# Moving a cast, a set of transposes and three output steps in a hand-ordered attention and MLP kernel

## The chip, the cores and the metric

The kernel runs on one core of a Trainium2 chip. The metric is the device time of one execution in microseconds (us). The engines are TensorE (PE in the profile, its weight loads PEld), VectorE (DVE), ScalarE (ACT), GpSimd (POOL) and SyncE (SP). They run side by side and wait for each other by semaphores; each executes its own instructions in the order in which the program gives them.

## The reference

Eight batches of eight heads, 576 positions, head size 64. Heads 0 to 3 see the last 32 positions, heads 4 to 7 the positions with the same remainder modulo 32. The attention's output, 4608 rows of 512, goes through an MLP with a squared ReLU.

```python
scores = scale * np.matmul(q, k.transpose(0, 1, 3, 2))
mask_local = (rel >= 0) & (rel < stride)
mask_strided = (rel >= 0) & (pos[None, :] % stride == pos[:, None] % stride)
attn = softmax(np.where(masks, scores, -1e9))
x = np.matmul(attn, v).transpose(0, 2, 1, 3).reshape(4608, 512)
out = np.maximum(x @ w_in, 0.0) ** 2 @ w_out
```

## The kernel before

The attention works on units: a unit is a pair of heads of one batch, numbered 4 * batch + pair; pairs 0 and 1 are local, 2 and 3 strided. Its output is written, transposed, into four tiles `xt`, which are the moving operand of the MLP.

The MLP runs in nine chunks of 512 rows. A chunk is 16 groups `mm1` (four 128x512 products into one PSUM bank, L734; the relu `r` on ScalarE, L740; its square `g_sb` on VectorE, L741) and then 16 groups `mm2` (four products, L756; each fourth group ends an output tile `y`, evicted by ScalarE, L760, and stored from SP's queue, L764). Groups are numbered on: chunk 0's mm1 is 0 to 15 (0 to 4 are done earlier), its mm2 16 to 31, chunk 1's mm1 32 to 47, and so on; chunk 3 is 96 to 127. So a group's number says what it is.

The order of the work is written out by hand in the string `PLAN`. A line `n: words` says which attention steps are issued ahead of group n, in the order of the words; then the group is issued, and then what earlier steps put off with `later` (masks, squares). There is no planner: the place of a word sets the order on every engine and on every queue that the step uses. The words that matter here:

- `c9ka`, `c9kv`: cast of unit 9's k (a reordering copy from the loaded tile to `k_l`, L303), on ScalarE (a) or VectorE (v). Batch 2's local units are 8 and 9, batch 3's 12 and 13.
- `T9kv`: six transposes of it on TensorE into a bank (L480), copied by VectorE to `kTl` (L487).
- `S8!`: scores of a local unit, 12 small products into four banks (L532), four exponentials on ScalarE (L548), two masks put off on VectorE (L554).
- `D8.0`, `D8.1`: the two halves of the product with V (L694), a reciprocal and a product on VectorE (L699, L700). `E17` transposes such an output by a DMA from SP's queue (L709).
- `A12k`: transposing DMA of the cast k from SP's queue (L391).
- `U5`: loads of the strided heads' v into `v_st` (one buffer) from POOL's queue (L417, L420). `B40v`, `B41v`: spread of batch 4's v over `vb`, even and odd columns, on VectorE (L424).
- `C5k`, `X5k`: load of the strided k from POOL's queue (L355) and its transposing DMA from SP's (L360) into `kT_s`. `k50v`, `k51v`: copies of it to `kb` on VectorE (L371, L374).
- `s4.0` to `s4.2`: scores of batch 4's strided heads in three parts (L601), exponential (L602), mask (L604). `x4.0` to `x4.2`: the sums and the products with V (L612, L615) into two banks, Ln and Exp on ScalarE (L617, L618), and then six, six and four products on VectorE that copy the scaled output into `xt` (L625, L631).
- `G4`, `G5`: the scores of both local units of a batch at once, 24 products into six banks (L577), six exponentials (L588), masks (L584). `H4v` shifts part of v (L437).

Banks: `mm1` and `mm2` take turns on two banks; the attention steps take the oldest of a ring of six. A step waits until the step that had its bank six places earlier has been read. G takes all six.

Of the kernel before, what the change touches and what calls it, by code (L numbers as in the profile page):

```python
# [45 lines left out]
28: V3 E5a x1.2  # L46
29: c8kv
30: c8qv
31: c9ka c9qv
33: T8kv  # L50
34: C3q T8qv
35: T9qa
36: T9kv
38: C3k S8!
39: c12kv A12k
40: c13kv A13k
41: D8.0
42: D8.1 S9!
44: k20v E8 c12qv A12q
45: k21v D9.0 c13qv A13q  # L60
46: B20v D9.1
# [25 lines left out]
81: x3.0  # L87
83: x3.1
85: x3.2
93: H4v  # L90
94: G4
95: k40v
96: k41v B40v
97: Y20 Y21 B41v
98: U5
99: X5k D16.0 D16.1
100: C6k
# [6 lines left out]
107: D17.0  # L104
109: Q24k Q24q D17.1 s4.2
110: B50v
111: x4.0 B51v
112: E17
113: k50v
114: k51v x4.1  # L110
117: x4.2
121: G5
124: V6
127: H5v
128: U6
# [897 lines left out]
```

## Time and profile before

| what | us |
|---|---|
| three runs | 299.83, 300.20, 300.69; median 300.20 |
| the profiled execution | 300.21, its span 298.3 |
| TensorE busy | 289.8 (97%) |
| VectorE busy | 179.5 (60%) |
| ScalarE busy | 171.3 (57%) |
| GpSimd busy | 72.7 (24%) |
| share of TensorE in the chain that ended last | 83% |
| share of VectorE, DMA, ScalarE in it | 7%, 4%, 3% |

A timeline row has the start in us, the time in us, the engine, the line, the operation, output and input tiles, the shapes and how many instructions were merged; in brackets stand the engine's idle time before it and what ended that. `psb` is PSUM. A row of PEld is a weight load; the loads of a group are 0.216 us apart when nothing stands between. A row of SPq or a POOL row with DMA is the issue of a transfer, not the transfer. The list of DMA issues gives the time from issue to landing.

### The profile page before, as it was taken

What the parts mean: (1) busy time and instruction counts of PE and PEld (TensorE: products, weight loads), DVE (VectorE), ACT (ScalarE), POOL (GpSimd) and SP (SyncE); (2) the same over time, 40 slices, a digit from 0 to 9 for tenths busy, and PEclk for the clock granted to TensorE, in tenths of its full rate; (3) what the DMA queues carried; (4) which work ended last, traced back from release to release, by engine and by line L of the source; (5) the groups of instructions that cost most, each with busy time, mean ns of one, the idle gap of its engine ahead of it and who ended that gap; (6) DMA issues with size and microseconds to landing.
All of it is one profiled execution on the core that took longest, in us unless ns stands there. A gap on an engine that the chain in (4) does not pass through costs nothing.

```text
span 298.3 us, 5623 instructions
## 1 busy us (share of the span) xinstructions
PE 289.8 (97%) x2112; PEld 145.3 (49%) x2148; DVE 179.5 (60%) x465; ACT 171.3 (57%) x321; POOL 72.7 (24%) x107
## 2 busy tenths in 40 slices
PE   7989999999999999999999999999999999999995
PEld 3644555544544444454455445544454444444444
DVE  5657679686788585689367945786475534004400
ACT  3758846775677636764477447645665256217511
POOL 8874742005503007136304800000000000000000
PEclk9999999999999999999999999999999999999999
DMA  8999999999999999999998999411011100011012
GB/s 159 179 210 202 193 198 185 154 185 211 157 167 183 132 154 191 147 155 185 195 139 120 175 174 144 81 55 73 35 23 55 70 37 0 35 70 38 0 70 70
DMA packets 91722, 37.36 MB, mean 125 GB/s; under 512 B 77548, under 2 KB 85830, under 8 KB 91696
## 3 DMA queue, kind: packets, MB, share of 16 engines
q0 software_dynamic: 50608, 18.33, 58.1%
q1 hardware_dynamic: 40944, 18.62, 32.4%
q8 instruction: 16, 0.26, 0.4%
q10 hardware_dynamic: 144, 0.07, 0.1%
q14 instruction: 10, 0.08, 0.1%
HBM read 37.22 MB, written 9.44 MB: 156 GB/s over the span
## 4 chain that ended last, share of the span: by engine, by line
PE 83%; DVE 7%; DMA 4%; ACT 3%; issue 2%; POOL 0%; DVEq 0%; POOLq 0%; ACTq 0%
PE psb L734 38%; PE psb L756 32%; DVE xt L625 2%; DMA kT_s<-k_t 2%; DMA k_l<-in_k_dram 2%; PE psb L694 2%; PE psb L791 1%; PE psb L480 1%; PE psb L532 1%; PE psb L781 1%; PE psb L601 1%; ACT r L740 1%; DVE g_sb L741 1%; PE psb L615 1%; PE psb L612 1%
## 5 line engine op out<-in xcount | busy, mean ns | idle before, releaser
L734 PE MATMUL psb<-xt,w_in_b 128*128 128x512 bf16 x557 | 132.8, 379 | 1.4 <-ACT r L740 0.2
L756 PE MATMUL psb<-w_out_b,g_sb 128*128 128x512 bf16 x543 | 125.7, 379 | 1.2 <-DVE g_sb L741 0.4
L740 ACT ACTIVATE r<-psb 128x512 bf16<-128x512 f32 x144 | 85.3, 599 | 38.8 <-PE psb L734 33.1
L741 DVE TENSOR_TENSOR g_sb<-r 128x512 bf16<-128x512 bf16 x144 | 60.6, 423 | 69.9 <-ACT r L740 68.9
L734 PEld LDWEIGHTS <-w_in_b 128*128 128x128 bf16 x576 | 53.1, 98 | 58.9 <-issue 1.9
L756 PEld LDWEIGHTS <-g_sb 128*128 128x128 bf16 x560 | 52.1, 98 | 59.1 <-DVE g_sb L741 1.1
L760 ACT COPY y<-psb 128x512 f32<-128x512 f32 x35 | 20.6, 590 | 52.1 <-PE psb L756 47.3
L625 DVE TENSOR_TENSOR xt<-psb,rv 64x144 bf16<-64x144 f32 x84 | 34.0, 405 | 10.5 <-ACT rv L618 9.4
L617 ACT ACTIVATE rv<-psb 128x432 f32<-128x432 f32 (+1 forms) x21 | 10.5, 501 | 12.8 <-PE psb L612 12.8
L700 DVE TENSOR_TENSOR x_l<-psb,rinv 96x384 bf16<-96x384 f32 x28 | 15.5, 553 | 1.0
L355 POOL DMA_DIRECT2D q_t<-in_q_dram x6 | 3.2, 538 | 47.4 <-DMA qT_s<-q_t 46.3
L602 ACT ACTIVATE e<-psb 128x432 bf16<-128x432 f32 (+1 forms) x21 | 10.4, 496 | 4.1 <-PE psb L601 4.1
L284 POOL DMA_DIRECT2D k_l<-in_k_dram x16 | 11.9, 748 | 2.8 <-ACT rv L618 2.0
L631 DVE TENSOR_TENSOR xt<-psb,rv 64x270 bf16<-64x270 f32 (+1 forms) x28 | 10.9, 431 | 2.5 <-ACT rv L618 2.2
L588 ACT ACTIVATE e<-psb 128x384 bf16<-128x384 f32 x24 | 9.6, 509 | 3.4 <-PE psb L577 3.4
L618 ACT ACTIVATE rv<-rv 128x432 f32<-128x432 f32 (+1 forms) x21 | 11.2, 533 | 0.7
L284 POOL DMA_DIRECT2D q_l<-in_q_dram x16 | 11.6, 728 | 0.0
L584 DVE TENSOR_TENSOR e<-e,mask_all 128x576 bf16<-128x576 bf16 x16 | 6.7, 456 | 8.0 <-ACT e L588 8.0
L694 PEld LDWEIGHTS <-e 128*128 128x128 bf16 x168 | 8.7, 101 | 5.0
L694 PE MATMUL psb<-vl,e 128*128 128x65 bf16 x168 | 9.5, 195 | 0.0
L355 POOL DMA_DIRECT2D k_t<-in_k_dram x6 | 3.2, 536 | 25.1 <-DMA kT_s<-k_t 23.1
L615 PEld LDWEIGHTS <-vb 128*128 128x128 bf16 x154 | 7.1, 97 | 3.8
(120 smaller groups left out, 218.6 us busy)
## 6 DMA issues: line engine op xcount, KB each, us to landing
out_dram<-y SPq DMA_DIRECT2D x35, 256.0 KB, 2.8
w_out_b<-in_moe_w_out_dram POOLq DMA_DIRECT2D x4, 512.0 KB, 15.4
q_t<-in_q_dram POOLq DMA_DIRECT2D x7, 288.0 KB, 7.4
k_t<-in_k_dram POOLq DMA_DIRECT2D x7, 288.0 KB, 7.1
vl<-in_v_dram POOLq DMA_DIRECT2D x6, 288.0 KB, 7.2
v_st<-in_v_dram POOLq DMA_DIRECT2D x7, 216.0 KB, 7.1
w_in_b<-in_moe_w_in_dram POOLq DMA_DIRECT2D x2, 704.0 KB, 14.3
k_l<-in_k_dram POOLq DMA_DIRECT2D x16, 72.0 KB, 7.0
```

Of the source, the lines that this page charges most:

```text
L284: nc.gpsimd.dma_start(out=t[:, :, hh, :], in_=src[b, 2 * p + hh].rearrange("(t p) d -> p t d", p=QL))
L617: nc.scalar.activation(rv, pn, AF.Ln)
L618: nc.scalar.activation(rv, rv, AF.Exp, scale=-1.0)
L625: nc.vector.tensor_tensor(to[:, :, NJ * part:NJ * (part + 1), par], of, by, op=ALU.mult)
L631: nc.vector.tensor_tensor(t, of[:, g:, :, lo:lo + k], by[:, g:, :, lo:lo + k], op=ALU.mult)
L694: nc.tensor.matmul(po[0:m, n, :], e[:, c:c + m], rhs[:, NL * part + n, 0:D + 1], start=True, stop=True)
L700: nc.vector.tensor_tensor(x, po[0:QL, :, 0:D], rinv[0:QL].to_broadcast([QL, NL, D]), op=ALU.mult)
L734: nc.tensor.matmul(ph, w_in_b[:, kk, 128 * ff:128 * (ff + 1)], xt[kk][:, 512 * c:512 * (c + 1)], start=(kk == order[0]), stop=(kk == order ...
L740: nc.scalar.activation(r, ph, AF.Relu)
L741: later(1, lambda: nc.vector.tensor_tensor(g[:, ff, :], r, r, op=ALU.mult))
L756: nc.tensor.matmul(py, g[:, ff, 128 * j:128 * (j + 1)], w_out_b[:, ff, :], start=(ff == 0), stop=(ff == 15))
L760: nc.scalar.copy(y, py)
```

## The change

Only the plan's text is changed. Line 31 has the cast of unit 9's k on VectorE. Its transposes go from ahead of group 36 to ahead of group 39, behind the cast of 12's k and its transposing DMA, and so behind the scores of unit 8. At group 42 the scores of unit 9 go ahead of the second half of unit 8's product with V. The spread of batch 4's v goes from 96 and 97 to 88 and 89. The three parts of batch 4's strided output go from 111, 114, 117 to 113, 115, 118; the second spread of batch 5's v goes from 111 to 114, the scores of batch 5's local units from 121 to 122. E17 goes from 112 to 111.

```diff
-31: c9ka c9qv
+31: c9kv c9qv
 33: T8kv
 34: C3q T8qv
 35: T9qa
-36: T9kv
 38: C3k S8!
-39: c12kv A12k
+39: c12kv A12k T9kv
 40: c13kv A13k
 41: D8.0
-42: D8.1 S9!
+42: S9! D8.1
...
+88: B40v
+89: B41v
 93: H4v
 94: G4
 95: k40v
-96: k41v B40v
-97: Y20 Y21 B41v
+96: k41v
+97: Y20 Y21
 98: U5
...
 109: Q24k Q24q D17.1 s4.2
 110: B50v
-111: x4.0 B51v
-112: E17
-113: k50v
-114: k51v x4.1
-117: x4.2
-121: G5
+111: E17
+113: k50v x4.0
+114: k51v B51v
+115: x4.1
+118: x4.2
+122: G5
```

## The prediction

> **What bounds the kernel now.** I read the busy line and the clock row first, then the chain of waits, then the timeline of each place that the change touches, one engine at a time.
>
> ```profile
> PE 289.8 (97%) x2112; PEld 145.3 (49%) x2148; DVE 179.5 (60%) x465; ACT 171.3 (57%) x321; POOL 72.7 (24%) x107
> ...
> PEclk9999999999999999999999999999999999999999
> ```
>
> TensorE is busy 97% of 298.3 us at the full granted clock, so nothing but its own waits can be gained or lost. The profiled execution took 300.21 us (span plus 1.91 outside it); the median of the three runs is 300.20, so a sum made on one holds for the other. I call 0.3%, 0.9 us, what a measurement can tell from no change.
>
> A group is four 128x512 products; its first weight loads, without other work between, are 0.863 us apart. Where a plan word stands between, the surplus is its price; a larger surplus is a wait. Four waits lie near the edited words. Around groups 31 to 33:
>
> ```profile
> 50.77 0.59 ACT L760 COPY y<-psb 128x512 f32<-128x512 f32 x1 [0.28 <-PE psb L756]
> 51.26 0.83 ACT L303 COPY k_l<-xt 96x768 bf16<-96x768 bf16 x1
> 51.38 0.36 DVE L303 COPY k_l<-xt 96x768 bf16<-96x768 bf16 x1
> 51.99 0.58 ACT L760 COPY y<-psb 128x512 f32<-128x512 f32 x1
> ...
> 52.09 0.10 PEld L480 LDWEIGHTS <-k_l 96*128 96x128 bf16 x1
> ...
> 52.62 0.41 PE L480 MATMUL psb<-ident,k_l 96*128 96x96 bf16 x6 [0.16 <-ACT y L760]
> ```
>
> The cast of 9's k sits on ScalarE between two evictions; the second ends at 52.57, and the transposes of 8's k, which take its bank, start only then. Around groups 38 to 44:
>
> ```profile
> 58.66 1.31 ACT L548 ACTIVATE e<-psb 128x288 bf16<-128x288 f32 x4
> 59.83 1.13 ACT L740 ACTIVATE r<-psb 128x512 bf16<-128x512 f32 x2
> ...
> 60.52 0.53 PEld L734 LDWEIGHTS <-w_in_b 128*128 128x128 bf16 x3 [0.47 <-issue]
> ...
> 64.99 0.53 PEld L734 LDWEIGHTS <-w_in_b 128*128 128x128 bf16 x3 [0.29 <-issue]
> ```
>
> S8's four exponentials hold up the relu of group 38; its bank is wanted by group 40, which stands until 60.5. Group 44 does the same behind S9. Around groups 110 to 122:
>
> ```profile
> 132.46 2.50 DVE L625 TENSOR_TENSOR xt<-psb,rv 64x144 bf16<-64x144 f32 x6 [0.59 <-ACT rv L618]
> 134.99 0.52 DVE L424 COPY vb<-v_st 54x1408 bf16<-54x1408 bf16 x1
> 135.54 0.42 DVE L741 TENSOR_TENSOR g_sb<-r 128x512 bf16<-128x512 bf16 x1
> ...
> 140.03 1.57 DVE L631 TENSOR_TENSOR xt<-psb,rv 64x270 bf16<-64x270 f32 x4
> ...
> 136.02 0.76 PEld L756 LDWEIGHTS <-g_sb 128*128 128x128 bf16 x5 [0.84 <-DVE g_sb L741]
> ...
> 140.96 0.41 PEld L577 LDWEIGHTS <-kTl 64*128 64x128 bf16 x18 [0.42 <-issue]
> 141.66 0.18 PEld L577 LDWEIGHTS <-kTl 64*128 64x128 bf16 x6 [0.29 <-issue]
> ```
>
> The square of group 111 (135.54) is queued on VectorE behind the six products of x4.0 and a spread, and group 115 waits for it. Then G5's last third waits until the products of x4.2 end at 141.60.
>
> **The change, part by part.** All starts are of first weight loads, in the clock of the trace before.
>
> *c9k from ScalarE to VectorE.* It takes 0.83 us from ScalarE and gives VectorE 0.35 (51.65 to 52.00 for the same shape). The last eviction can then start when its product is done: earlier ones start 0.41 to 0.42 after the next group's first load (49.49 to 49.91, 50.36 to 50.77), so 51.22 gives 51.64, and its end 52.22. The transposes load at 52.09, and a transpose follows its load by 0.22 (53.52 to 53.74): 52.31 in place of 52.62, a gain of 0.31. Bounds: 0 (were the eviction not early) and 0.32, the whole surplus. On VectorE the cast goes ahead of 9's q, which is read at 54.4, and falls into an idle stretch of 0.86 before 53.13; without that cover it would delay the square of group 32 by 0.35, which is first read at group 48.
>
> *T9k behind S8.* A set of transposes costs TensorE 0.26: groups with one between start 1.12 apart (53.95, 55.08), 0.86 without. Ahead of S8 it is paid in full. After group 38 it lies in front of group 40's wait, which is 0.355 (60.52, where 59.95 + 0.216 was due) and ends with the relu of 38; that follows S8, so it moves by 0.31 + 0.26, and the wait shrinks to 0.10. Gain 0.26; bounds 0 and 0.26. Its 0.75 us copy on VectorE is now queued behind the square of 38 and the cast of 12's k (whose load lands at 58.08, needed at 60.3) and ends at 61.3 (square at 60.50 - 0.57, then steps of 0.34, 0.27 and 0.75). S9's loads come 1.00 after group 41's (86.71 to 87.71 at group 66), 61.53 - 0.57 + 1.00 = 61.96, so 0.6 to spare. Behind the copy wait a mask, three squares, 13's cast and the outputs of D8.0 and D8.1; with the steps of the trace (0.37, 0.34 each, 0.27, 0.70 each) S9's first mask ends at 64.8, against 65.07 (65.64 - 0.57) when D9.0 loads it: the next to be late. The transposes take the bank of 8's q, S8 one bank earlier in the ring; all were emptied before.
>
> *S9 before D8.1.* S9's exponentials cannot start before the relu of group 41 leaves ScalarE (62.64 to 63.24, they start at 63.13), so group 44's wait of 0.17 stays: 0, between 0.17 gained and 0.17 lost, since D8.1 then follows with its masks long ready.
>
> *V's spread of batch 4 to 88 and 89.* Two copies of 0.52 on VectorE leave 116.7 and 118.4 and go behind x3.2's products and ahead of the shift at 109.64. VectorE then idles 0.74 for the k of batch 4 (110.87) and 3.76 before 115.15; the k goes 0.3 later and is read after 123. No TensorE wait ends on the copies: 0; were the cover gone, 1.04 us on G4's masks, first read after 118.6. They also free v_st: the two loads of batch 5's v on POOL's queue, at 119.26 after a wait of 1.18 for the second copy, can go at 118.1. No DMA issue changes its place in either queue.
>
> *x4 and G5.* With x4.0 out of the way before group 111, group 112 starts at 131.27 (130.40 + 0.863). Its square is ready at 132.7 and is read at 135.3: the first wait, 0.53 (134.65 to 136.03 is 1.39 for 0.86), goes. VectorE then runs k50v at 132.75 to 133.5; x4.0 stands after group 112, its Ln starts 1.46 after that group's first load (132.52 to 133.98), 132.73, and its products 1.15 after that (131.31 to 132.46), 133.88. Then six products 2.50, k51v 0.80, the spread 0.55, six 2.50, four 1.57: the end is 141.8, against 141.60 before. G5, one group later, would reach its last third at 141.67 (131.27; nine groups 7.77; x4's parts 0.40, 0.40 and 0.30, the surplus of groups 110-111, 113-114 and 116-117; the group with G5 1.79, as G4's; less 0.25 from the last third to the next group) and waits until 141.9: 0.22 of wait, where the second wait had been 0.34. Gain 0.53 + 0.34 - 0.22 = 0.65; bounds 0.86, with no wait left, and 0.3, if VectorE is 0.35 slower. E17's DMA, moved from 112 to 111, keeps its place in SP's queue: it is issued at 132.47, when E16's, at 130.48, lets it.
>
> Sum: 0.31 + 0.26 + 0 + 0 + 0.65 = 1.22 us. After group 123 I find no wait of TensorE in the trace of before that could take it back; DMAs land early (batch 4's k at 110.84 for use after 123, qT of batch 5 at 134.07 for use at 154). 300.2 - 1.2 = 299.0.
>
> **The rivals.**
>
> *One half only.* If the head start of 0.57 is lost again before group 64, since VectorE is nearly without gaps from 65 to 72 (the chain runs along it there) and the copy of T9k now sits just ahead, the time is 300.2 - 0.65 = 299.55. Against it: the last square is ready at 71.57 and its weight load is at 72.60. If instead the x4 stretch stays bound by VectorE, 300.2 - 0.57 = 299.6; for it: VectorE is busy 14.45 of 17 us there.
>
> *Nothing moves.* TensorE meets the next late releaser in both places: 300.2. For it, only that each wait removed here had another engine close behind; the margins above (0.6, 0.3, 1.0 us) speak against it.
>
> *Slower: k50v in front of x4.0.* It now heads the queue that G5 waits for, and reads a DMA transpose issued at 126.79.
>
> ```profile
> 119.26 0.54 POOL L417 DMA_DIRECT2D v_st<-in_v_dram  x1 [1.18 <-DVE vb L424]
> ...
> kT_s<-k_t SPq DMA_TRANSPOSE x1, 4.0
> ...
> 131.33 0.53 POOL L355 DMA_DIRECT2D k_t<-in_k_dram  x1 [10.89 <-DMA kT_s<-k_t]
> ```
>
> It landed after 4.0 us, at 130.78, and k50v would start at 132.75, or 132.2 with the head start; another 0.35 is spare before x4.0's products. Other transposes of this tile took up to 11.2. At 11.2 it would land at 138.0, x4.0 would start at 138.8, 4.9 later, and the whole time would be 300.2 - 1.2 + 4.9 = 303.9. It costs something from a landing 1.75 us late, and decides the sign from 2.9 us late. For it: the v loads, 1.2 us earlier, share the DMA engines with the five transposes issued one after another from 121.50 on. Against it: those loads end at 126.27 even now, before this transpose is issued, and the next load is issued only after it has landed. The Trainium skill, page "DMA: Bandwidth & Descriptors", section "Issuing engines are not separate DMA queues", says that DMAs of all issuing engines run on the same 16 DMA engines and interleave. By that rule an earlier load slows the transposes ahead of this one; the trace agrees that company costs, with 10.2 us for the same transpose at 53.06 among loads and 4.0 alone.
>
> **How the numbers follow.** Both gains hold: 0.64, 299.0, own range 298.6 (no wait left, and 0.17 at group 44) to 299.4. One half only: 0.16, 299.6. Nothing: 0.06, 300.2. Slower: 0.14, up to 303.9; for such a shuffle many small releasers can come late, so I give it more than the margins alone would. The range 298.6 to 300.2 leaves out the slower case and a little below. Faster by over 0.3% (below 299.3): 0.64 and 0.02 of the halves, 0.66; within: 0.14 + 0.06, 0.20; slower: 0.14.
>
> **What would show it.** The transposes after group 32 start at their load plus 0.22 with no wait on the eviction; group 40's wait is near 0.1; group 115 has none; the products of x4.0 start 1.4 later against group 110 and G5's last third waits 0.2 for x4.2. Wrong would be: VectorE idle before k50v, S9 waiting for kTl, D9.0 waiting for its mask, or G5 standing longer than before.

## The result and the profile after

| | before | changed |
|---|---|---|
| median of six runs, us | 300.27 | 299.09 |
| lowest and highest | 299.83, 300.69 | 298.81, 299.58 |
| span of the profiled execution | 298.3 | 297.7 |
| its own time | 300.21 | 299.36 |

The ratio is 0.9962, with a 95% interval of 0.9949 to 0.9975: 1.1 us less, between 0.75 and 1.5. The forecast was 299.0. In later runs some executions, of the kernel before as of the others, had a lower granted clock and took about 2% longer; the ratios and medians leave them out.

The two spans differ by 0.6 only, and the starts of the groups tell why. I read the first weight load of each group in both traces (first loads, as in the prediction) and take the difference. Group 20, which no edit touches, starts 0.87 later in this profiled execution: its chain of waits begins with a load of v that the other's does not have.

```profile
5.53 8.30 DMA vl<-in_v_dram
13.83 0.02 issue
13.85 0.49 DVE vl L438
```

That is not the change: over the fourteen traces of this study, whose programs do not differ up to group 30, group 32 starts between 0.04 earlier and 0.77 later than in the first trace. So starts are compared from group 32 on, set to zero there. The changed kernel then stands like this against the one before:

| group | 33 | 39 | 41 | 45 | 110 | 123 | 283 |
|---|---|---|---|---|---|---|---|
| us | -0.32 | -0.14 | -0.58 | -0.58 | -0.58 | -1.38 | -1.38 |

Three steps, 0.32, 0.26 and 0.80, each at a place that the prediction named, and nothing is given back after. (At 39 the moved transposes have just been issued, and the wait that they shorten comes in group 40. Line numbers of the changed kernel are one higher; those of the other kernels shift with the number of lines in their plans.) First, the timeline of the changed kernel around group 32:

```profile
51.55 0.59 ACT L761 COPY y<-psb 128x512 f32<-128x512 f32 x1 [0.28 <-PE psb L757]
...
52.41 0.59 ACT L761 COPY y<-psb 128x512 f32<-128x512 f32 x1 [0.28 <-PE psb L757]
...
52.71 0.35 DVE L304 COPY k_l<-xt 96x768 bf16<-96x768 bf16 x1
52.86 0.49 PEld L481 LDWEIGHTS <-k_l 96*128 96x128 bf16 x6
...
53.08 0.42 PE L481 MATMUL psb<-ident,k_l 96*128 96x96 bf16 x6
```

The last eviction waits for its product now (0.28 of idle, PE), not for the cast; the transposes follow their load by 0.22 without a wait. Then the weight loads of groups 38 to 44:

```profile
58.62 0.55 PEld L735 LDWEIGHTS <-w_in_b 128*128 128x128 bf16 x4
59.28 0.48 PEld L481 LDWEIGHTS <-k_l 96*128 96x128 bf16 x6
...
60.72 0.53 PEld L735 LDWEIGHTS <-w_in_b 128*128 128x128 bf16 x3 [0.21 <-issue]
...
62.73 0.28 PEld L533 LDWEIGHTS <-kTl 64*128 64x128 bf16 x12 [0.42 <-DVE e L555]
...
65.19 0.53 PEld L735 LDWEIGHTS <-w_in_b 128*128 128x128 bf16 x3 [0.29 <-issue]
```

9's transposes lie after group 38, and the idle time in group 40 is 0.21 where it was 0.47; that of group 44 is 0.29 as before. Last, VectorE and the weight loads from group 111 to 122:

```profile
132.51 0.43 DVE L742 TENSOR_TENSOR g_sb<-r 128x512 bf16<-128x512 bf16 x1 [0.20 <-ACT r L741]
132.85 0.37 DVE L372 COPY kb<-kT_s 64x864 bf16<-64x864 bf16 x1
133.14 0.26 DVE L375 COPY kb<-kT_s 64x324 bf16<-64x324 bf16 x1
134.08 2.50 DVE L626 TENSOR_TENSOR xt<-psb,rv 64x144 bf16<-64x144 f32 x6 [0.68 <-ACT rv L619]
136.62 0.38 DVE L372 COPY kb<-kT_s 64x864 bf16<-64x864 bf16 x1
136.92 0.24 DVE L375 COPY kb<-kT_s 64x324 bf16<-64x324 bf16 x1
137.19 0.52 DVE L425 COPY vb<-v_st 54x1408 bf16<-54x1408 bf16 x1
137.74 2.51 DVE L626 TENSOR_TENSOR xt<-psb,rv 64x144 bf16<-64x144 f32 x6
140.28 1.58 DVE L632 TENSOR_TENSOR xt<-psb,rv 64x270 bf16<-64x270 f32 x4
```

```profile
135.04 2.28 PEld L757 LDWEIGHTS <-g_sb 128*128 128x128 bf16 x12
...
141.49 0.60 PEld L578 LDWEIGHTS <-kTl 64*128 64x128 bf16 x24 [0.42 <-issue]
```

The square of group 111 is done at 132.94, long before group 115 wants it, and its loads (within the twelve from 135.04) run through. The first copies of k lie ahead of 0.68 of idle time; the last products end at 141.86; G5's 24 loads come in one row, without the break before the last six. A little of that wait is left: the group with G5 takes 1.84, against 1.79 in two kernels below where VectorE is done earlier (fill, G5 only). In the kernel before, all four copies of k lay between the square and the products of x4.1, and two of them took long:

```profile
135.89 0.37 DVE L371 COPY kb<-kT_s 64x864 bf16<-64x864 bf16 x1
136.18 0.49 DVE L374 COPY kb<-kT_s 64x324 bf16<-64x324 bf16 x1
136.68 0.38 DVE L371 COPY kb<-kT_s 64x864 bf16<-64x864 bf16 x1
136.98 0.51 DVE L374 COPY kb<-kT_s 64x324 bf16<-64x324 bf16 x1
```

### The profile page after: what moved, and what is told of

Read it like the earlier page. It is cut to its first block, busy times and chain, and to the rows that moved or that the text cites. A ratio compares the mean times of both kernels' runs of the same rounds, so it can differ in the third digit from the quotient of the medians.

```text
span 297.7 us, 5623 instructions
## 1 busy us (share of the span) xinstructions
PE 289.2 (97%) x2112; PEld 145.1 (49%) x2148; DVE 180.2 (61%) x466; ACT 170.9 (57%) x320; POOL 72.8 (24%) x107
## 4 chain that ended last, share of the span: by engine, by line
PE 93%; DMA 3%; issue 1%; DVE 1%; POOL 1%; DVEq 0%; POOLq 0%
PE psb L735 42%; PE psb L757 40%; DMA vl<-in_v_dram 3%; PE psb L695 2%; PE psb L616 1%; PE psb L602 1%; PE psb L782 1%; PE psb L613 1%; PE psb L578 1%; PE psb L533 1%; PE psb L481 1%; POOL xt L297 0%; DVE xt L663 0%; PE psb L328 0%; DVE x_l L683 0%
## 5 line engine op out<-in xcount | busy, mean ns | idle before, releaser
L618 ACT ACTIVATE rv<-psb 128x432 f32<-128x432 f32 (+1 forms) x21 | 10.5, 501 | 14.0 <-PE psb L613 14.0
```

Source lines behind the costliest of these rows:

```text
L618: nc.scalar.activation(rv, pn, AF.Ln)
```

## The experiments

The theory: TensorE is the bound; the gain is its own waits, each taken away in its place, and the last stretch hangs on the end of x4.2's products on VectorE. The table has all runs: starts against the kernel before, zero at group 32, in us; the last column is taken before rounding.

| kernel | 33 | 45 | 110 | 123 | gained 110 to 123 |
|---|---|---|---|---|---|
| changed, two profiles alike | -0.32 | -0.58 | -0.58 | -1.38 | 0.80 |
| first half | -0.32 | -0.58 | -0.57 | -0.67 | 0.10 |
| cast only | -0.32 | -0.31 | -0.32 | -0.66 | 0.34 |
| transposes only | 0.00 | -0.26 | -0.25 | -0.47 | 0.22 |
| second half | 0.00 | 0.00 | 0.00 | -0.84 | 0.84 |
| G5 only | 0.00 | 0.00 | 0.01 | -0.32 | 0.33 |
| no swap | -0.32 | -0.57 | -0.56 | -1.27 | 0.70 |
| batch 4's spread late | -0.32 | -0.58 | -0.57 | -1.13 | 0.55 |
| k50v behind x4.0 | -0.32 | -0.58 | -0.58 | -0.62 | 0.04 |
| G5 at 121 | -0.32 | -0.57 | -0.57 | -0.52 | -0.05 |
| k late | -0.32 | -0.57 | -0.57 | +1.87 | -2.44 |
| fill | -0.32 | -0.74 | -1.00 | -1.86 | 0.86 |

Where no time is given below, the kernel ran once (298.69 to 300.44). One run can't tell such steps, since 23 runs of the kernel before lay between 299.52 and 302.85; the starts are read, from one profile each.

The last column has a part that no edit made. The first half, the cast alone and the transposes alone change nothing between groups 110 and 123, and yet gain 0.10, 0.34 and 0.22 there. G5's own wait differs: from group 120 to 121 it takes 2.12 in the trace of before, 2.00, 1.79 and 1.82 in these three. With the cast alone only one of the four copies of k is long, VectorE is done earlier, and G5 doesn't wait:

```profile
135.66 0.37 DVE L371 COPY kb<-kT_s 64x864 bf16<-64x864 bf16 x1
135.96 0.23 DVE L374 COPY kb<-kT_s 64x324 bf16<-64x324 bf16 x1
136.20 0.54 DVE L371 COPY kb<-kT_s 64x864 bf16<-64x864 bf16 x1
136.67 0.23 DVE L374 COPY kb<-kT_s 64x324 bf16<-64x324 bf16 x1
...
140.74 0.54 PEld L577 LDWEIGHTS <-kTl 64*128 64x128 bf16 x24 [0.42 <-issue]
```

So up to 0.34 of a gain there hangs on the one trace of before, which has the longest of these waits. The wait of group 115, 0.53 there, is between 0.52 and 0.61 in all four.

**The two halves.** The first has lines 31, 36, 39 and 42 of the change alone, the second its lines from 111 on.

```diff
 first half, against before
-31: c9ka c9qv
+31: c9kv c9qv
-36: T9kv
-39: c12kv A12k
-42: D8.1 S9!
+39: c12kv A12k T9kv
+42: S9! D8.1
```

> The plan of before with the cast, 9's transposes and the swap at 42 alone. My theory (the gain is waits of TensorE taken away, each in its place): group 33 starts 0.32 earlier against group 21 than before, group 41 0.58 earlier, and this stays to the end; group 115 and G5 wait as before (0.53 and 0.34). Time 0.58 less, about 299.7. Rival (the head start is lost again at the next late releaser): group 64 or group 123 starts as before, time unchanged.

The median is 299.49 against 300.27, ratio 0.9976, interval 0.9961 to 0.9990: 0.7 us less. By the starts it is 0.58 up to group 110 and 0.67 at the end. The head start is there at group 33 and 41 and is kept to the end; the rival falls.

```diff
 second half, against before
-111: x4.0 B51v
-112: E17
-113: k50v
-114: k51v x4.1
-117: x4.2
-121: G5
+111: E17
+113: k50v x4.0
+114: k51v B51v
+115: x4.1
+118: x4.2
+122: G5
```

> The plan of before with x4's three parts, batch 5's second spread, E17 and G5 moved alone; batch 4's spread stays at 96 and 97. My theory: nothing changes up to group 110; group 123 starts 0.65 to 0.80 earlier; time 0.65 to 0.8 less, about 299.5. Rival (the spread of batch 4, which lets POOL's loads go earlier, made part of this gain): the copies of batch 5's k at 136 to 138 take 0.5 each beside POOL's issues, as before, G5 waits 0.2, and the gain is 0.65 and not 0.80.

The starts give 0.84, so the gain does not need the early spread of batch 4. The times missed the expected 299.5: 300.06 against 300.27, with a ratio of 0.9992 (0.9969 to 1.0016). They can neither show nor deny the gain, since 0.84 us and no gain at all both lie within the interval.

**The steps of the first half, one at a time.**

```diff
 cast only, against before
-31: c9ka c9qv
+31: c9kv c9qv
```

> The plan of before with 9's k cast on VectorE alone. My theory: the eviction ahead of the transposes starts at its product, the transposes lose their wait, group 33 starts 0.32 earlier against group 21, and group 41 as well, since everything up to group 40's wait hangs on TensorE. Rival (ScalarE was not what held them, the wait moves to another bank or the cast of 8's k): less than 0.1.

```diff
 transposes only, against before
-36: T9kv
-39: c12kv A12k
+39: c12kv A12k T9kv
```

> The plan of before with 9's transposes behind S8 alone. My theory: group 38 starts 0.26 earlier, group 39 as before, the wait in group 40 shrinks from 0.36 to 0.10, and group 41 starts 0.26 earlier. Rival (S9 waits for the late copy of 9's k, or D9.0 for its mask): group 42 or 45 gives 0.26 or more back.

```diff
 no swap, against the changed kernel
-42: S9! D8.1
+42: D8.1 S9!
```

> The changed kernel with D8.1 ahead of S9 again. My theory: the relu of group 41 sets S9's exponentials, so group 44's wait stays at 0.17 in either order and group 45 starts within 0.03 of the changed kernel. Rival: the swap takes something off group 44, and it comes back here, up to 0.17.

0.31, 0.26 and 0.01 at group 45, each as expected; 0.31 and 0.26 add up to the first half's 0.58 but for 0.01. The weight loads of the kernel with the transposes alone show the mechanism: the set after group 38, and 0.21 of idle time in group 40.

```profile
58.45 0.54 PEld L733 LDWEIGHTS <-w_in_b 128*128 128x128 bf16 x4
59.11 0.49 PEld L479 LDWEIGHTS <-k_l 96*128 96x128 bf16 x6
59.54 0.79 PEld L733 LDWEIGHTS <-w_in_b 128*128 128x128 bf16 x5
60.55 0.53 PEld L733 LDWEIGHTS <-w_in_b 128*128 128x128 bf16 x3 [0.21 <-issue]
```

**The second half, taken apart.**

```diff
 G5 at 121, against the changed kernel
-122: G5
+121: G5
```

> The changed kernel with G5 back at 121. My theory (VectorE's end of x4.2 ties G5): x4's late start only moves the wait from group 115 into G5; G5's last third waits 0.8 to 0.9, group 123 starts 0.8 to 0.86 later than in the changed kernel, about as in the kernel before against group 41. Rival (the gain is that of group 115 alone): 0.3 later at most.

```diff
 G5 only, against before
-121: G5
+122: G5
```

> The plan of before with G5 one group later and nothing else. My theory: G5's wait (0 to 0.34 in the traces with x4 in its old place) goes, group 115's wait of 0.53 stays: 0 to 0.34 gained at group 123. Rival (G5's place is what counts): 0.5 or more.

With x4 late and G5 in its old place nothing is gained (-0.05). The weight loads of that kernel show where the 0.53 of group 115 went: the loads of groups 115 to 117 run through, and G5 stands instead.

```profile
134.62 2.28 PEld L757 LDWEIGHTS <-g_sb 128*128 128x128 bf16 x12
...
140.21 0.41 PEld L578 LDWEIGHTS <-kTl 64*128 64x128 bf16 x18 [0.42 <-issue]
141.49 0.18 PEld L578 LDWEIGHTS <-kTl 64*128 64x128 bf16 x6 [0.86 <-issue]
```

G5 alone has no wait, and that of group 115 stays. Its gain of 0.33 is no measure of the move, since the cast alone gains as much there with G5 in its old place. With x4 late the move of G5 is worth 0.85 (0.80 against -0.05), and the products of x4.2 end as late in both kernels (10.40 and 10.39 after the start of group 112). So neither of the two moves gives the 0.80 by itself; they give it together, since both waits end on the same row of work on VectorE.

```diff
 k50v behind x4.0, against the changed kernel
-113: k50v x4.0
+113: x4.0 k50v
```

> The changed kernel with the first copies of batch 5's k (k50v) behind x4.0 in place of ahead of it. My theory (they lie in the idle 0.68 that VectorE has before x4.0's products, and G5 is tied to the end of x4.2's): x4.0's products start as before, all behind them 0.6 later, G5's last third waits 0.5 to 0.6, so group 123 starts 0.5 to 0.6 later than in the changed kernel. Rival (G5 isn't tied to VectorE any more): no change.

```diff
 batch 4's spread late, against the changed kernel
-88: B40v
-89: B41v
-96: k41v
-97: Y20 Y21
+96: k41v B40v
+97: Y20 Y21 B41v
```

> The changed kernel with batch 4's spread back at 96 and 97. If the spread is worth nothing to TensorE: every group starts as in the changed kernel, 0.80 gained from 110 to 123. If it works through POOL's queue: the v loads go again after the second copy, POOL's later issues are 1 to 2 us later, at least one copy of batch 5's k takes 0.5 and not 0.24, and G5 waits 0.1 to 0.3.

Both lose, 0.76 and 0.25. The first is the expected loss of the idle time, and more than expected, since one copy also took 0.51. The second is as much as was expected if the spread works through POOL's queue, but the second half has the same late spread and loses nothing. What decides is the end of x4.2's products, counted from the start of group 112:

| kernel with x4 late, G5 at 122 | end of x4.2's products after group 112's start | gained 110 to 123 |
|---|---|---|
| second half | 10.36 | 0.84 |
| changed | 10.40 | 0.80 |
| no swap | 10.50 | 0.70 |
| batch 4's spread late | 10.65 | 0.55 |
| k50v behind x4.0 | 11.16 | 0.04 |

In all five the two numbers add up to 11.20: an end 0.1 later is a wait 0.1 longer. The ends differ by VectorE's copies in that row. In the kernel with the late spread they were, on VectorE:

```profile
132.25 0.52 DVE L370 COPY kb<-kT_s 64x864 bf16<-64x864 bf16 x1
132.70 0.22 DVE L373 COPY kb<-kT_s 64x324 bf16<-64x324 bf16 x1
133.49 2.50 DVE L624 TENSOR_TENSOR xt<-psb,rv 64x144 bf16<-64x144 f32 x6 [0.56 <-ACT rv L617]
136.02 0.52 DVE L370 COPY kb<-kT_s 64x864 bf16<-64x864 bf16 x1
136.47 0.23 DVE L373 COPY kb<-kT_s 64x324 bf16<-64x324 bf16 x1
136.72 0.68 DVE L423 COPY vb<-v_st 54x1408 bf16<-54x1408 bf16 x1
```

0.52 for 0.38 and 0.68 for 0.52 behind x4.0: 0.30 in sum, about the 0.25 that the end is later. Long copies run beside POOL's issues (below), and the times of these differ between executions of one kernel: in the two profiles of the changed kernel, whose groups 98 start within 0.04 of each other, POOL issues the same load of q_t at 132.79 and at 130.66. Whether the place of batch 4's spread has a part in it, one profile of each kernel can't show.

**The slower rival.** 

```diff
 k late, against the changed kernel
-99: X5k D16.0 D16.1
-100: C6k
+99: D16.0 D16.1
-111: E17
+111: E17 X5k C6k
```

> The changed kernel with the transposing DMA of batch 5's k, and the load behind it, put off from 99 and 100 to 111, behind E17 in SP's queue; this tests the slower rival of the prediction. It is then issued 5 to 7 us later and lands about 4 us after that, near 136 on the old clock. My theory: VectorE stands at k50v until then, x4.0's products start 2.5 to 4 later, G5's last third waits as much, and the kernel is 1.5 to 3 slower than the one before. Rival (G5's tie to VectorE is loose): under 1 lost.

One run took 304.34 against a median of 300.11: 4.2 slower, 3.55 by the starts of the last groups. VectorE of that kernel:

```profile
131.81 0.42 DVE L741 TENSOR_TENSOR g_sb<-r 128x512 bf16<-128x512 bf16 x1 [0.44 <-ACT r L740]
135.96 0.65 DVE L371 COPY kb<-kT_s 64x864 bf16<-64x864 bf16 x1 [3.72 <-DMA kT_s<-k_t]
136.53 0.22 DVE L374 COPY kb<-kT_s 64x324 bf16<-64x324 bf16 x1
136.68 2.51 DVE L625 TENSOR_TENSOR xt<-psb,rv 64x144 bf16<-64x144 f32 x6
```

It stands 3.72 us at k50v, until the DMA lands. The products of x4.0 start 3.29 later against group 112 than in the changed kernel, and the group with G5 takes 3.24 longer. So the tie is real. In the changed kernel the DMA landed at 129.06 and k50v ran at 132.85, so the rival did not come about there. At group 123 the kernel is 1.87 slower than the one before, within my 1.5 to 3. The total was larger by something I had not thought of: after the wait TensorE's mean granted clock was 0.55 for 3.8 us, and groups 123 to 125 lose 1.69 more. The windows of the same kernel (length; busy time and number of instructions for TensorE, its weight loads, VectorE, ScalarE and GpSimd; then the granted clock, the DMA share and GB/s):

```profile
140.00:144.70 4.70, 1.78 (x29) 0.83 (x26) 4.53 (x12) 0.98 (x2) 2.25 (x3) 1.00 1.66 213
145.20:149.00 3.80, 3.80 (x11) 1.38 (x10) 1.78 (x4) 1.82 (x5) 0.00 (x0) 0.55 0.81 101
149.00:153.00 4.00, 4.00 (x20) 1.86 (x19) 0.00 (x0) 0.92 (x2) 0.00 (x0) 1.00 0.18 67
```

**The changed kernel once more, and the same idea at the waits that were left.** The changed kernel was run again beside a version with four more moves.

```diff
 fill, against the changed kernel
-41: D8.0
-42: S9! D8.1
+42: S9! D8.0 D8.1
-66: Y17 D12.0
-67: Y16 S13! C5q
+66: Y17
+67: Y16 S13! C5q D12.0
-93: H4v
-94: G4
+93: H4v G4
-114: k51v B51v
+114: k51a B51v
```

> The changed kernel once more, to compare the next one with it and to see a second profile. My theory: the shift of TensorE's starts against the kernel before is again 0.32 at group 33, 0.26 by group 41, and between 0.5 and 0.85 from 110 to 123, the last by how many of VectorE's copies in that stretch fall beside POOL's issues. Time 1.1 to 1.4 less than before.

> The changed kernel with four more moves of the same kind: D8.0 behind S9, D12.0 behind S13, G4 one group earlier, batch 5's second k copy on ScalarE. My theory (work that TensorE owes anyway, put in front of a wait, costs nothing there): the waits of group 44 (0.17), 69 (0.17) and 97 (0.10) go, G5 has none, and TensorE ends 0.4 to 0.5 earlier than in the changed kernel; time 0.4 less. Rival (the masks of S9 or S13 come late, or x4.1's logarithm waits behind the copy on ScalarE): D9.0, D13.0 or group 115 take 0.2 or more back.

The changed kernel's second profile has the steps of the first to 0.01, and a ratio of 0.9956 (0.9932 to 0.9981). The other version gains 0.17 by group 45, 0.17 more by group 70, 0.09 more by group 98 and 0.05 more by 123: 0.48 over the changed kernel, as expected, and nothing is taken back. Its weight loads at groups 66 to 69:

```profile
86.73 0.28 PEld L531 LDWEIGHTS <-kTl 64*128 64x128 bf16 x12 [0.42 <-issue]
87.09 0.26 PEld L693 LDWEIGHTS <-e 128*128 128x128 bf16 x6
87.26 0.58 PEld L733 LDWEIGHTS <-w_in_b 128*128 128x128 bf16 x4
87.95 0.43 PEld L693 LDWEIGHTS <-e 128*128 128x128 bf16 x6
88.32 2.72 PEld L733 LDWEIGHTS <-w_in_b 128*128 128x128 bf16 x14
```

D12.0 follows the scores, and the fourteen loads from 88.32 run on through group 69, which waited 0.17 before. Its median is 298.86 (11 runs), against 299.45 for the changed kernel (9) and 300.11 for the one before (20). The ratio to the one before is 0.9951 (0.9927 to 0.9974), whose interval overlaps the changed kernel's; that it is faster than the changed kernel rests on the starts, and on medians 0.6 apart.

## Why the prediction was right, and where it was off

- The cast: 0.31 forecast, 0.32 measured by itself (group 33). The releaser was the eviction, as read.
- The transposes: 0.26 forecast and measured by itself; the wait in group 40 is 0.10 as forecast (60.72 less 60.41 and 0.216). The margins held and were a little wider than worked out: the copy of 9's k ends at 62.05 and S9 loads at 62.73, 0.68 for 0.6; S9's first mask ends at 65.44 and D9.0 loads at 65.83, 0.39 for 0.27.
- The swap: 0 forecast, 0.01 measured. The exponentials start at 63.33 in the changed kernel, within the last 0.11 of the relu of group 41 (62.84 to 63.44), as before.
- The spread of batch 4 and the earlier loads: nothing on TensorE, as forecast. The v loads went at 116.27 without a wait, earlier than the 118.1 of the prediction, since the issues ahead of them were earlier too; the transposing DMA of batch 5's k took 3.9 us, against 4.0. (That 4.0 was without loads, but not alone: four transposes issued before it landed between 126.82 and 128.57.) The prediction took earlier loads to slow the transposes ahead of this one. They came out the other way: the four took 4.8, 4.1, 3.3 and 2.6, against 5.3, 4.5, 3.8 and 3.1 before, and the loads were over by 124.04, against 126.27. In the two kernels with the late spread, whose loads of v were issued within 0.8 of the first transpose, that one took 7.5 and 7.1. The Trainium skill, page "DMA: Bandwidth & Descriptors", section "Issuing engines are not separate DMA queues", says that DMAs of all issuing engines run on the same 16 DMA engines and interleave; these times agree with that.
- x4 and G5: 0.65 forecast, 0.80 measured against the trace of before. This is the one term that was mis-sized. The step that was off is the end of x4.2's products, put at 141.8 on the old clock, 10.5 us after group 112: it was 10.40. I took k51v at 0.80 from the row of before; it took 0.57, since two of the copies of before had run long beside POOL's issues, and of the 0.22 of wait that was to be left in G5 only 0.05 came. In two of the variants, with a copy or two drawn out, 0.16 and 0.30 did. The second wait, 0.34, was also taken from one trace as if it were fixed; in the three kernels that leave this stretch alone it is 0.21, 0 and 0.03. Against the cast alone, which has none, the 0.80 would be 0.46.
- The sum: 1.22 forecast, 1.38 by the starts, 1.1 (0.75 to 1.5) by the times. That the forecast time and the median agree to 0.1 is in part luck: the interval is wider than that, and so is the spread of G5's wait from trace to trace. How large that wait is in the runs without a profile is not shown.
- The rivals. "One half only" fell with the starts of the two halves. "Slower" fell since the DMA landed early, and its mechanism was shown by the kernel with a late k. It priced a late start of x4.0 one for one; that kernel lost 3.24 for a start 3.29 later, and another 1.69 with the clock, which the price left out.

## What to carry to other kernels

When one engine is busy 97% of the time, compare the spacing of its repeated groups with the spacing of undisturbed ones: each surplus is either work with a price or a wait with a releaser, and only the second can be taken away. Work that this engine owes anyway is free in front of a wait, and two waits that end on the same row of another engine's work must be removed together, or one takes over from the other. Where such a row ends just as it is wanted, its length must be taken from instructions that ran undisturbed, and the wait behind it from more than one trace.

## What the runs showed of the hardware

**VectorE's plain copies are drawn out beside POOL's DMA issues.** Over all fourteen traces, from 60 us on, 326 copies from SBUF to SBUF (`kb` in its two shapes, `vb`, the shift of `vl`) did not overlap a DMA issue on GpSimd: none took more than 0.384 and 0.242 (`kb`), 0.523 and 0.486 us. Of 246 that overlapped one, 91 took longer, up to 0.92. Of VectorE's operations with two inputs (squares, masks, the products that read PSUM), 922 overlapped one, and none took over 0.006 longer than the longest of its shape that did not. These are observations across kernels; no run moved POOL's issues by themselves. The Trainium skill, page "SBUF — State Buffer", section "SBUF: two separate sides", says that VectorE and GpSimd share one pair of ports, which the operation that starts first holds alone for its whole length, and that an operation of VectorE takes it when it runs in a two-port mode, or with two inputs in SBUF against a GpSimd operation that reads SBUF. The counts agree with that if the copies ran in such a mode, which no run shows.

**TensorE's granted clock fell without one long gap.** In the kernel with the late k TensorE was busy 1.78 of the 4.70 us from 140.0 to 144.7, with idle stretches of 1.68 and 1.25 before the later parts of G5's products, and then the granted clock was 0.55 from 145.2 to 149.0. The Trainium skill, page "TensorE: Matmul & The Clock Gate", section "HAM oscillation — how this bites in real kernels", gives "no PE-idle gaps >~3.4µs" as the abstract rule; here the clock fell after two shorter gaps with a little work between. It was seen in one execution.
